# Batch 3's v as float32 from SyncE's queue, and chunk 0's output stores issued later, in a fused attention and MLP kernel

## The chip, the cores and the metric

The kernel runs on one core of a Trainium2 chip. The metric is the device time of one execution in microseconds. Three timed runs of the kernel before took 263.56, 263.73 and 264.59 us, median 263.73.

The core's engines are named as in the profile: PE (TensorE, matrix products; PEld is its weight load), DVE (VectorE), ACT (ScalarE), POOL (GpSimd) and SP (SyncE, which only issues DMAs). Each runs its own list of instructions in order and waits on semaphores of the others. POOL issues DMAs too, and only those of POOL convert float32 to bfloat16 on the way. All DMAs run on the same 16 DMA engines.

## The reference

Inputs q, k and v have the shape (8 batches, 8 heads, 576 rows, 64 columns). The attention has no product of q and k; its output is normalized and goes through an MLP with a residual:

```python
q_s = softmax(q, axis=-1)
k_s = softmax(k, axis=2)
kv = np.einsum('bhsd,bhse->bhde', k_s, v)
x = np.einsum('bhsd,bhde->bhse', q_s, kv)       # then (8, 576, 512)
xn = (x - mean(x)) / np.sqrt(var(x) + 1e-06) * g_ln
out = x + np.maximum(xn @ w_ch1, 0.0) @ w_ch2   # 512 -> 2048 -> 512
```

The output is float32.

## The kernel before

The 576 rows of a batch are split into 512 main rows (four tiles of 128) and 64 remainder rows. The work is cut into nine chunks: chunk c below 8 is the main rows of batch c, chunk 8 (`C9`) collects the remainder rows of all batches. While PE does the MLP of chunk c, the attention of batch c+1 and the loads and exponentials of batch c+2 run beside it.

**The order is written by hand.** `run` (L846) walks through the MLP steps of a chunk, `mlp_steps` (L811); each has a weight, and the running sum of weights is the position. A list of side steps, pairs of a position and a function, is merged into it: a side step is emitted when the sum reaches its position. So a position fixes where an instruction stands in its engine's list. `second_side` (L891) holds the side steps of chunk 1, `attn_fast` (L877) and `prep_fast` (L866) those of later chunks, and the loop at L1171 adds the rest. SP's DMAs, DVE's and POOL's work all follow this order.

**The MLP** of chunks from 2 on uses a scheme of seven products in place of eight (`mm1_fast`, L753, and `mm2_fast`, L684). The first layer's products are numbered; product 1 writes a PSUM bank bx, product 5 a bank bb, product 6 goes on in bx, product 2 in bc, product 7 in bx, product 3 in bb and product 4 in bx. Each is done for two groups of columns, one after the other. ACT copies bx into bc (L774) after product 1 and bb into s (L778) after product 5. DVE's L781 adds bx and s into bb after product 6; its L784 adds bx and s into hT after product 7. ACT's L792 writes the rectified results. Products 5, 6, 7 and 4 take tq as an operand: four differences of quarters of the transposed x, made two instructions each by `sum_x` (L235; L247 on POOL).

**Loads.** `load_v` (L139) loads v of a batch from POOL as bfloat16 into a tile vt of one buffer, and the remainder rows of v in two small DMAs (L149). For batch 3 it first issues a four-element copy on POOL (L143), which waits until the first pair of batch 2's x transposes has landed. `cast_v` (L131) copies half of v at a time into vm, the layout with a column of ones that the k-v product takes; DVE does it at L137, ACT at L135. `load_batch` (L1108) loads q and k on SP; for batch 3's q it waits, through a four-element conversion on POOL (L1115), until batch 2's query transposes have landed, for others through a DVE memset (L1113). q lies in the tile tag qt with two buffers in turn.

**Transposes.** `eq_T` (L259) transposes a batch's exponentiated q into eqT, and `xn_T` (L262) two of the four tiles of x at a time into xnT; both are DMA transposes on SP (L255), whose queue keeps its order.

**Stores.** `y_out` (L514) finishes a tile of chunk 0 on DVE (L518, tile ot of four buffers) and issues its store at once on POOL (L524). From chunk 1 on, `y_quarter` (L604) does the same at L609 and L615, in the same four buffers.

Of the kernel before, what the change touches and what calls it, by code (L numbers as in the profile page):

```python
# [12 lines left out]
FP32 = mybir.dt.float32  # L13
# [7 lines left out]
def kernel(  # L21
# [16 lines left out]
    nc = tc.nc  # L38
# [5 lines left out]
    T = 4  # L44
# [56 lines left out]
    def main_src(x, b, h0, hn):  # L101
        return x[b, h0 : h0 + hn, 0:SM, :].rearrange("h (p t) d -> p h (t d)", t=T)
# [28 lines left out]
    def cast_v(b, j, eng=None):  # L131
        hs = slice(4 * j, 4 * j + 4)
        dst = vm[:, b % 2, :, hs, 0:D].rearrange("p t h d -> p h t d")
        if eng is nc.scalar:
            nc.scalar.copy(dst, vts[b][:, hs])  # L135
        else:
            nc.vector.tensor_copy(out=dst, in_=vts[b][:, hs])  # L137

    def load_v(b, after=None):  # L139

        vts[b] = mlp.tile([P, H, T, D], BF16, tag="vt", name="vt", bufs=1)
        if after is not None:
            nc.gpsimd.tensor_copy(out=vts[b][0:1, 0, 0, 0:4], in_=after)  # L143
        if b == 1:
            load_krem(nc.gpsimd, b)
        nc.gpsimd.dma_start(vts[b].rearrange("p h t d -> p h (t d)"), main_src(v, b, 0, H))
        for half in range(2):
            hs = slice(4 * half, 4 * half + 4)
            nc.gpsimd.dma_start(  # L149
                vr[SR * half : SR * half + SR, b % 2, hs, 0:D],  # L150
                v[b, hs, SM:S, :].transpose([1, 0, 2]),
            )
# [340 lines left out]
    def mm1_part(c, m, t0, tn, ko):  # L493
# [13 lines left out]
        if m % 2 == 1 and at + tn == 2 and ko == KO1 - 1:  # L507
# [3 lines left out]
            else:  # L511
                nc.scalar.activation(dst, ph, AF.Relu)

    def y_out(c, t, pc, cols=slice(0, 512), eng=None):  # L514
        if cols.start == 0:
            hbox["ot"] = outp.tile([P, DM], FP32, tag="ot", name="ot")
        ot = hbox["ot"][:, cols]
        nc.vector.scalar_tensor_tensor(  # L518
            ot, in0=pc, scalar=rstds[c][:, t : t + 1], in1=xs[c][0][:, t, cols],
            op0=ALU.mult, op1=ALU.add,  # L520
        )
        eng = eng or nc.gpsimd
        if c < B:
            eng.dma_start(  # L524
                out[c, 0:SM, :].rearrange("(p t) n -> p t n", t=T)[:, t, cols], ot
            )
        else:
            for half in range(2):
                eng.dma_start(
                    out[2 * t + half, SM:S, cols], ot[64 * half : 64 * half + 64]  # L530
                )

    def mm2(c, t, ko):
        if ko == 0:
# [356 lines left out]
    def second_side():  # L891

        s = [(p, lambda i=i: quarter_w2(i, 1)) for i, p in enumerate((13, 16, 44, 46))]
        s += [(8, lambda: xn_pT(1, 2, nc.scalar)), (12, lambda: xn_pT(1, 3, nc.vector))]
        s += [(3, lambda: exp_q(2, 0, 4)), (9, lambda: exp_q(2, 2, 4)), (14, lambda: eq_T(2))]
        s += [(42, lambda: square_sum(1, 2)), (67, lambda: square_sum(1, 3)), (71, lambda: rstd_op(1))]
        s += [(14.1, lambda: load_batch(3, (2,), eqTs[2][0:1, T - 1, NP - 1, 0:4])), (31, lambda: load_batch(3, (0,)))]
        s += [(18 + 2 * j, lambda j=j: cast_v(2, j)) for j in range(2)]
        s += [(60.5, lambda: load_v(3, xnTs[2][0:1, 1, KO1 - 1, 0:4]))]
        s += [(15 + 3 * t, lambda t=t: reduce_q(2, t, 2)) for t in (0, 2)]  # L900
        s += [(36, lambda: recip_q(2))]
        s += [(18, lambda: exp_k(2, 0, 4)), (22, lambda: exp_k(2, 2, 4)), (26, lambda: prep_kvrem(2))]
        s += [(41, lambda: kv_all(2))]
        s += [(46, lambda: start_x(2))]
        for t, (p0, p1) in enumerate(((52, 54), (57, 59), (62, 65), (70, 74))):
            s += spread([lambda t=t, i=i: po_mm(2, t, i) for i in range(NP)], p0, p1)
            s += [(p1, lambda t=t: x_fast(2, t)), ((73, 82, 88, 94)[t], lambda t=t: square_sum(2, t))]
        s += [(60, lambda: xn_T(2, 0, 2)), (77, lambda: xn_T(2, 2, 2)), (100, lambda: rstd_op(2))]
        s += [(75, lambda: exp_q(3, 0, 4)), (79, lambda: exp_q(3, 2, 4)), (85, lambda: eq_T(3))]
        s += [(97, lambda: exp_k(3, 0, 4)), (108, lambda: exp_k(3, 2, 4)), (113, lambda: prep_kvrem(3))]  # L910
        s += [(p, lambda i=i: sum_w1(i, 1)) for i, p in ((2, 28), (3, 30))]
        s += spread([lambda i=i: sum_x(2, i) for i in range(4)], 95, 108)
        return s
# [207 lines left out]
    with tc.manual_schedule(  # L1121
        engines={mybir.EngineType.PE, mybir.EngineType.DVE, mybir.EngineType.Activation,
                 mybir.EngineType.SP, mybir.EngineType.Pool}
    ):
        first_batch()
        load_behind(1, (2,))
        load_w2(8, 2)
        load_behind(1, (0,))
        load_w2(10, 2)
        load_behind(1, (1,))  # L1130
        load_w2(12, 2)
        load_w2(14, 2)
        load_behind(2)

        def po_x(c, t):
            for i in range(NP):
                po_mm(c, t, i)
            x_fast(c, t)

        run(  # L1140
            mlp_steps(0),
            [
                (2, lambda: (q0_rest(2), x_fast(0, 2))),
                (2.5, lambda: (eq_pT(0, 3, nc.scalar), x_plain(0))),
                (6, lambda: (q0_rest(3), x_plain(1))),
                (7.5, lambda: (xn_pT(0, 2, nc.vector), x_fast(0, 3))),
                (16, lambda: xn_pT(0, 3, nc.vector)),
                (22, lambda: square_sum(0, 0)),
                (26, lambda: square_sum(0, 1)),
                (30, lambda: square_sum(0, 2)),  # L1150
                (34, lambda: square_sum(0, 3)),
                (38, lambda: rstd_op(0)),
            ]
            + [(70, lambda: exp_q(1, 0, 4)), (72, lambda: exp_q(1, 2, 4))]
            + [(75 + t, lambda t=t: reduce_q(1, t)) for t in range(T)]
            + [((82, 86, 94, 98)[t], lambda t=t: eq_pT(1, t, nc.scalar)) for t in range(T)]
            + [(84, lambda: nc.vector.reciprocal(eqs[1][2], eqs[1][1]))]
            + [(88, lambda: exp_k(1, 0, 4)), (92, lambda: exp_k(1, 2, 4))]
            + [(26 + 4 * i, lambda i=i: scale_w1(i % KO1, i // KO1)) for i in range(2 * KO1)]
            + [(p, lambda i=i: quarter_w2(i, 0)) for i, p in enumerate((60, 62, 64, 66))]  # L1160
            + [(p, lambda i=i: sum_w1(i, 0)) for i, p in enumerate((80, 84, 88, 92))]
            + [(p, lambda i=i: sum_w1(i, 1)) for i, p in enumerate((96, 98))]
            + [(103 + 0.4 * j, lambda j=j: cast_v(1, j)) for j in range(2)]
            + [(104.5, lambda: prep_kvrem(1))]
            + [(112, lambda: (kv_all(1), start_x(1)))]
            + [(118, lambda: (po_x(1, 0), po_x(1, 1)))]
            + [(123, lambda: xn_pT(1, 0, nc.scalar)), (125, lambda: square_sum(1, 0))]
            + [(124.1, lambda: (po_x(1, 2), po_x(1, 3)))]
            + [(126, lambda: xn_pT(1, 1, nc.scalar)), (127, lambda: square_sum(1, 1))]
        )  # L1170
        for c in range(1, B):  # L1171
            side = []
            if c == 1:
                side += second_side()
            else:
                if c + 1 < B:
                    side += attn_fast(c + 1)
                else:
                    side += attn_rest()
                    side += [(6 + i, lambda i=i: sum_x(c, i)) for i in (2, 3)]  # L1180
                if c + 2 < B:
                    side += [(1, lambda b=c + 2: load_batch(b))]
                    side += [(26, lambda b=c + 2: load_v(b))]
                    side += prep_fast(c + 2)
            if c == 2:
                side += [(19 + j, lambda j=j: cast_v(3, j)) for j in range(2)]
            if c == B - 2:
                side += [(1, load_qrem)]
                side += spread([lambda r=r: exp_qrem(r) for r in range(T)], 58, 80)
                side += [(84, lambda: eq_T(C9))]  # L1190
            sums = [(57, 0)] if c == FAST else [(p, i) for i, p in enumerate((30, 41))]
            run(mlp_steps(c), side + [(at, lambda i=i: sum_h(0, i)) for at, i in sums])
        run(mlp_steps(C9), [(33 + 3 * i, lambda i=i: sum_h(0, i)) for i in range(2)])
# [30 lines left out]
```

## Time and profile before

One execution was profiled. Its own time is 264.16 us, 0.43 above the median of the three timed runs; its span, the time that the trace covers, is 262.4 us, at a granted TensorE clock of 1.00.

| what | us |
|---|---|
| median of three timed runs | 263.73 |
| profiled execution, device time | 264.16 |
| its span | 262.4 |
| chunk 2's first product starts | 75.65 |
| batch 2's query transposes: issued, landed (8.0 later) | 51.73, 59.7 |
| batch 3's q on SP: issued, landed (5.7 later) | 60.25, 66.0 |
| batch 2's x transposes, first pair: issued, landed (7.9 later) | 63.95, 71.9 |
| chunk 0's four stores: first and last issue | 47.19, 52.38 |
| batch 3's v on POOL: issued, landed (6.4 later) | 73.28, 79.7 |

A line of a timeline gives the start in us, the time, the engine, the source line, the operation, the tiles written and read, their shapes, and how many instructions are merged. A bracket at the end gives how long the engine was idle before it, and what ended that. Rows of matmuls overlap at their ends, so how late PE is shows in the distance from start to start rather than in the busy time. For DMAs the profile has the issue, on the engine that issues (SPq, POOLq), and the time from issue to landing.

### The profile page before, as it was taken

The page shows a single profiled execution, that of the slowest core. Times are in us where ns is not written, and L with a number is a line of the kernel's source. Part 1 is how long each engine was busy: PE and PEld are TensorE (multiplying, and loading weights), DVE is VectorE, ACT ScalarE, POOL GpSimd, SP SyncE. Part 2 cuts the span into 40 slices and gives each one's busy share as a digit, 9 for nine tenths or more (in the row PEclk, how much of TensorE's full clock was granted, in tenths as well). Part 3 has the DMA queues.
Part 4 walks back from the last instruction along what each step waited for, and adds up shares of the span by engine and source line. Part 5 has one row for each costly group of instructions (what it writes and reads, how often), then busy time and mean ns, then how long its engine had stood idle before and what let it go on. Part 6 is the DMA issues. An engine that isn't in the chain of part 4 may idle for free.

```text
span 262.4 us, 6846 instructions
## 1 busy us (share of the span) xinstructions
PE 256.4 (98%) x2711; PEld 217.4 (83%) x2711; DVE 217.2 (83%) x482; ACT 180.7 (69%) x357; POOL 78.4 (30%) x130
## 2 busy tenths in 40 slices
PE   8999999999999999999999999999999999999993
PEld 5789755866888998899889988998899888888882
DVE  5676786988969997989798979997999889977873
ACT  4778670996967788678867886788678377447400
POOL 8752345200089008600860067008200300030000
PEclk9999999999999999999999999999999999999999
DMA  6999999995999964899489967997804620621014
GB/s 231 250 202 206 321 236 320 272 144 181 243 161 288 289 98 92 227 305 136 86 248 289 135 84 205 327 143 143 260 1 80 174 74 5 77 104 58 0 42 120
DMA packets 69895, 45.00 MB, mean 172 GB/s; under 512 B 41508, under 2 KB 66088, under 8 KB 69864
## 3 DMA queue, kind: packets, MB, share of 16 engines
q0 software_dynamic: 20368, 22.29, 38.8%
q1 hardware_dynamic: 48896, 21.76, 38.7%
q10 hardware_dynamic: 600, 0.53, 0.6%
q8 instruction: 21, 0.34, 0.5%
q14 instruction: 10, 0.08, 0.1%
HBM read 36.70 MB, written 9.44 MB: 176 GB/s over the span
## 4 chain that ended last, share of the span: by engine, by line
PE 92%; DMA 3%; POOL 1%; DVE 1%; issue 1%; ACT 0%; POOLq 0%; DVEq 0%
PE ba L598 19%; PE bx L750 18%; PE bb L750 9%; PE ph L501 8%; PE pc L547 5%; PE bc L750 5%; PE bc L598 5%; PE be L598 5%; PE bb L598 5%; DMA xnT<-xn 3%; PE ph L486 3%; PE warm L864 3%; PE po L417 2%; PE pkv L381 2%; PE ptr L933 1%
## 5 line engine op out<-in xcount | busy, mean ns | idle before, releaser
L598 PEld LDWEIGHTS <-hs 128*128 128x128 bf16 x512 | 49.6, 98 | 5.7
L750 PEld LDWEIGHTS <-w_q 128*128 128x128 bf16 x448 | 43.1, 98 | 5.6 <-issue 0.7
L598 PEld LDWEIGHTS <-hT 128*128 128x128 bf16 x392 | 37.3, 98 | 4.4
L750 PEld LDWEIGHTS <-w1g 128*128 128x128 bf16 x336 | 32.3, 98 | 4.0
L247 POOL TENSOR_TENSOR tq<-xnT 128x256 bf16<-128x256 bf16 x20 | 13.0, 666 | 64.4 <-DMA xnT<-xn 48.9
L598 PE MATMUL ba<-w_q,hs 128*128 128x256 bf16 x256 | 31.7, 273 | 0.0
L750 PE MATMUL bx<-tq,w_q 128*128 128x256 bf16 x224 | 29.0, 273 | 0.2 <-ACT s L778 0.2
L615 POOL DMA_DIRECT2D out_dram<-ot x28 | 15.3, 555 | 45.9 <-DVE ot L609 45.9
L431 ACT ACTIVATE scrap<-x,mv 128x512 bf16<-128x512 bf16 x36 | 26.0, 721 | 1.8 <-DVE x L447 1.4
L447 DVE SCALAR_TENSOR_TENSOR x<-po,rq 128x512 bf16<-128x512 f32 x34 | 23.3, 684 | 1.3 <-PE po L417 1.2
L774 ACT COPY bc<-bx 128x512 f32<-128x512 f32 x28 | 15.2, 595 | 13.0 <-PE bx L750 13.0
L781 DVE TENSOR_TENSOR bb<-bx,s 128x512 f32<-128x512 f32 x28 | 18.2, 694 | 6.8 <-ACT s L778 6.7
L792 ACT ACTIVATE hT<-bc 128x512 bf16<-128x512 f32 x28 | 15.3, 595 | 12.0 <-PE bc L750 12.0
L209 DVE TENSOR_REDUCE zq<-eq 128x16 f32<-128x1024 bf16 (+1 forms) x20 | 20.8, 1051 | 1.3 <-ACT eq L192 1.2
L578 DVE TENSOR_TENSOR hs<-hT 128x1024 bf16<-128x1024 bf16 x32 | 20.9, 674 | 0.9 <-ACT hT L792 0.5
L792 ACT ACTIVATE hT<-bb 128x512 bf16<-128x512 f32 x28 | 15.2, 595 | 8.4 <-PE bb L750 8.4
L784 DVE TENSOR_TENSOR hT<-bx,s 128x512 bf16<-128x512 f32 x28 | 18.1, 684 | 2.9 <-PE bx L750 2.9
L417 PE MATMUL po<-kv_sb,eqT 128*128 128x128 bf16 x120 | 20.2, 219 | 0.0
L623 ACT COPY s<-ba 128x512 f32<-128x512 f32 x15 | 8.7, 579 | 11.9 <-PE ba L598 7.3
L598 PE MATMUL ba<-w_sb,hT 128*128 128x256 bf16 x128 | 16.7, 273 | 0.0
L598 PE MATMUL bb<-w_q,hs 128*128 128x256 bf16 x128 | 16.5, 273 | 0.0
L778 ACT COPY s<-bb 128x512 f32<-128x512 f32 x28 | 15.6, 622 | 0.6 <-PE bb L750 0.5
(150 smaller groups left out, 543.8 us busy)
## 6 DMA issues: line engine op xcount, KB each, us to landing
out_dram<-ot POOLq DMA_DIRECT2D x32, 256.0 KB, 6.0
qt<-in_q_dram SPq DMA_DIRECT2D x5, 1024.0 KB, 6.9
kt<-in_k_dram SPq DMA_DIRECT2D x5, 1024.0 KB, 13.5
vt<-in_v_dram POOLq DMA_DIRECT2D x7, 512.0 KB, 13.4
qt<-in_q_dram POOLq DMA_DIRECT2D x2, 1024.0 KB, 12.6
kt<-in_k_dram POOLq DMA_DIRECT2D x2, 1024.0 KB, 14.7
kt<-in_k_dram SPq DMA_DIRECT2D x4, 288.0 KB, 4.6
w_raw<-in_moe_w_ch_dram POOLq DMA_DIRECT2D x4, 256.0 KB, 9.2
```

The lines of the kernel that those rows point to most:

```text
L209: nc.vector.reduce_sum(eqs[c][1][:, ts], eqs[c][0][:, ts], axis=AX.X)
L417: nc.tensor.matmul(pobox["p"][:, i * P : i * P + P], eqTs[c][:, t, i, :], kv_sb[:, c, i, :], start=True, stop=True,)
L431: nc.scalar.activation(scrap, x[:, t], AF.Square, bias=mv[:, t, 0:1], scale=-float(DM), accum_out=mv[:, t, 1:2],)
L447: nc.vector.scalar_tensor_tensor(x[:, t].rearrange("p (h d) -> p h d", h=H), in0=pobox[c, t].rearrange("p (h d) -> p h d", h=H), scalar=1. ...
L501: nc.tensor.matmul(ph[:, m % 2, at : at + tn], (w1g if c else w1_sb)[:, ko, m * P : (m + 1) * P], xnTs[c][:, t0 : t0 + tn, ko, :], start=( ...
L578: nc.vector.tensor_tensor(out=dst, in0=x, in1=y, op=op)
L598: nc.tensor.matmul(dst, lhsT, rhs, start=first and (own or t == 0) and k == 0, stop=k == KH - 1, skip_group_check=True)
L750: nc.tensor.matmul(dst[:, q], lhsT, rhs, start=first and q == 0 and ko == 0, stop=ko == 1, skip_group_check=True)
L778: nc.scalar.copy(at[g, "s"], at[g, "b"])
L781: nc.vector.tensor_tensor(out=at[g, "b"], in0=at[g, "x"], in1=at[g, "s"], op=ALU.add)
L784: nc.vector.tensor_tensor(out=h_out(g, 1, 1), in0=at[g, "x"], in1=at[g, "s"], op=ALU.add)
L792: nc.scalar.activation(h_out(g, odd, half), at[g, name], AF.Relu)
```

## The change

It has four parts.

- Batch 3's v is no longer loaded by `load_v` on POOL. `load_v32` loads it as float32 on SP, at position 78 of chunk 1, behind the second pair of x's transposes (position 77), into a tile of the tag qt. That tag's two buffers go round one place further for the later batches. The four-element copy on POOL goes.
- The two remainder loads of batch 3's v stay on POOL, in a function of their own, and are issued at position 14.3 of chunk 1 in place of 60.5.
- The casts of batch 3's v, both on DVE at positions 19 and 20 of chunk 2, come at position 4 on DVE and 10 on ACT, from float32.
- Chunk 0's four stores are held back in a list and issued on POOL at position 14.2 of chunk 1, right behind the conversion (14.1) that waits for batch 2's query transposes.

```diff
-    def load_v(b, after=None):
+    def load_v(b):
         vts[b] = mlp.tile([P, H, T, D], BF16, tag="vt", name="vt", bufs=1)
-        if after is not None:
-            nc.gpsimd.tensor_copy(out=vts[b][0:1, 0, 0, 0:4], in_=after)
         if b == 1:
             load_krem(nc.gpsimd, b)
         nc.gpsimd.dma_start(vts[b].rearrange("p h t d -> p h (t d)"), main_src(v, b, 0, H))
+        load_vrem(b)
+
+    def load_v32(b):
+        vts[b] = raw.tile([P, H, T, D], FP32, tag="qt", name="vt32")
+        nc.sync.dma_start(vts[b].rearrange("p h t d -> p h (t d)"), main_src(v, b, 0, H))
+
+    def load_vrem(b):
         for half in range(2):
...
+    late = []
+
     def y_out(c, t, pc, cols=slice(0, 512), eng=None):
...
-        if c < B:
+        if c == 0:
+            late.append((t, ot))
+        elif c < B:
...
+    def store_late():
+        for t, ot in late:
+            nc.gpsimd.dma_start(
+                out[0, 0:SM, :].rearrange("(p t) n -> p t n", t=T)[:, t, :], ot
+            )
...
-        s += [(60.5, lambda: load_v(3, xnTs[2][0:1, 1, KO1 - 1, 0:4]))]
+        s += [(14.2, store_late), (14.3, lambda: load_vrem(3)), (78, lambda: load_v32(3))]
...
-                side += [(19 + j, lambda j=j: cast_v(3, j)) for j in range(2)]
+                side += [(4, lambda: cast_v(3, 0)), (10, lambda: cast_v(3, 1, nc.scalar))]
```

## The prediction

> **What bounds the kernel now.** I read the page's busy times first, then the chain that ended last, and then the timelines of each engine around the one place where TensorE (PE) is late.
>
> ```profile
> span 262.4 us, 6846 instructions
> PE 256.4 (98%) x2711; PEld 217.4 (83%) x2711; DVE 217.2 (83%) x482; ACT 180.7 (69%) x357; POOL 78.4 (30%) x130
> PE 92%; DMA 3%; POOL 1%; DVE 1%; issue 1%; ACT 0%; POOLq 0%; DVEq 0%
> ```
>
> PE is busy 98% of the span at full granted clock, and 92% of the chain is PE. So a change to loads and stores can gain only where PE is late, and it loses wherever it makes PE late anew. The timeline of PE shows the late place, at the start of chunk 2:
>
> ```profile
> 75.65 1.04 PE L750 MATMUL bx<-xnT,w1g 128*128 128x256 bf16 x8
> 76.83 1.03 PE L750 MATMUL bb<-tq,w_q 128*128 128x256 bf16 x8
> 78.07 1.03 PE L750 MATMUL bx<-tq,w_q 128*128 128x256 bf16 x8 [0.21 <-ACT s L778]
> 78.94 1.04 PE L750 MATMUL bc<-xnT,w1g 128*128 128x256 bf16 x8
> ...
> 81.56 1.16 PE L750 MATMUL bx<-tq,w1g 128*128 128x256 bf16 x8
> 82.56 0.27 PE L750 MATMUL bx<-xnT,w1g 128*128 128x256 bf16 x1
> ```
>
> The first column is the start. Undisturbed, a row of eight follows the last after 0.87 us (78.07 to 78.94; in chunk 3, 102.66 to 103.53). Here the steps are 1.18, 1.24 and 1.00 us: PE loses 0.31, 0.37 and 0.13, together **0.81 us**. Elsewhere after 60 us PE's rows join, but for about 0.2 us around each batch's small attention matmuls, which stays. POOL's timeline names the cause of the first two:
>
> ```profile
> 71.98 0.18 POOL L143 COPY vt<-xnT 1x4 bf16<-1x4 bf16 x1 [11.76 <-DMA xnT<-xn]
> 73.28 0.91 POOL L146 DMA_DIRECT2D vt<-in_v_dram  x1 [1.12 <-issue]
> 74.18 1.28 POOL L149 DMA_DIRECT2D vr<-in_v_dram  x2
> 75.44 1.34 POOL L247 TENSOR_TENSOR tq<-xnT 128x256 bf16<-128x256 bf16 x2
> 76.71 1.31 POOL L247 TENSOR_TENSOR tq<-xnT,tq 128x256 bf16<-128x256 bf16 x2
> ```
>
> Product 5 multiplies by tq's first difference, ready at 76.78, and starts at 76.83; product 6 by the second, ready at 78.02, and starts at 78.07. PE's bracket names ACT's L778, but product 6 does not write the bank that L778 copies; the dates fit POOL. POOL was late because, from the landing of x's first transposes (72.0), it issued batch 3's v for 3.4 us before the differences. The third loss, 0.13, is VectorE's (DVE's): its cast of v (81.06, 0.42 us) stands ahead of the second L784, which ends at 82.07; product 4 of group 1 restarts at 82.13.
>
> **The change, part by part.**
>
> *v's load leaves POOL.* Gone ahead of the differences are the copy and its gap (1.30 us from 71.98 to 73.28), the load's issue (0.91) and two remainder issues (1.28). What is late next is the second pair of x's transposes: issued when the first issue ends at 68.9 and landing 3.7 us later (DMA issues by window), 72.7. From there, at 1.27 us a difference, the four are ready at 73.9, 75.2, 76.5 and 77.8. PE wants them at 76.5, 77.4, 79.15 and 80.9 (75.65 plus 1, 2, 4 and 6 rows of 0.875). Slack is 2 us or more even if the transposes land no earlier. Gain 0.68 us.
>
> *Chunk 0's four stores move.* Their issues (0.54 to 0.57 us each, 2.2 us) go from 47.2–52.9 to behind POOL's cast that waits for batch 2's query transposes (59.75), with v's remainder issues (1.28) behind them; POOL then has nothing until 72. Those transposes now land 8.0 us after issue beside the stores; the next two sets of that size take 4.3 each. So I expect them at about 56.0 in place of 59.7, and batch 3's q, k and the stores all to start some 3.7 us earlier. The stores put 1 MB beside q's and k's 2 MB: at some 330 GB/s (the DMA view from 62 us on) that is 3 us more, so the queue ahead of x's transposes empties about when it does now, or 1 us sooner. q is read by ACT at 66.45 and lands at 66.0; started 3.7 us earlier with at most 3 us of store traffic in the way, it is in time. The store tiles are written again by L609 at 70.73; issued at 56.5 to 58.7 and landing 6.0 to 8 us later, they are free. Cost zero; without that cover see rival C.
>
> *v in float32 on SP's queue.* One issue (0.4 us) behind the second pair of x's transposes, whose issue ends at 70.6 or sooner. Behind it on SP stand batch 3's query transposes (70.71 now, first read by PE at 87.8), then q, k and k's remainder of batch 4, which wait for DVE until 77.8 anyway; 1 MB more (3 us) is covered by over 9 us. Landing: q's 1 MB loads took 5.7 us (issued 60.25) and 6.9 (issued 77.9), so v is there by 76.3 to 77.5. The buffer taken is q's of batch 2, read out by ACT at 51.7; batch 4's q goes to the other, which batch 3's q leaves at 68.4. The cast now asks for v at 77.86.
>
> *The casts.* DVE's two (0.42 and 0.47, at 81.06 and 82.45) go: that returns 0.13. One comes at position 4, behind the memsets, into this hole:
>
> ```profile
> 76.64 1.21 DVE L209 TENSOR_REDUCE zq<-eq 128x16 f32<-128x1024 bf16 x1
> 77.79 0.06 DVE L1113 MEMSET qt<- 1x1 f32 x1
> 77.79 0.06 DVE L1113 MEMSET kt<- 1x1 f32 x1
> 78.76 1.30 DVE L781 TENSOR_TENSOR bb<-bx,s 128x512 f32<-128x512 f32 x2 [0.91 <-ACT s L778]
> ```
>
> No row has DVE copy float32 to bf16 from SBUF. The bounds are 0.42 (the bf16 copy of 1024) and 1.20 (the reduction of 1024). I take 0.68, the 1024-element bf16 TENSOR_TENSOR of L561, because it reads as many bytes per element. Queued behind it are L781's two adds, and product 7 of each group writes the bank that they read. With POOL on time they would be ready at 78.09 (chunk 3: 105.10 less 102.66, plus 75.65). The cast holds them to 78.5; they end at 79.2 and 79.8; product 7 wants its banks at 79.15 and 79.59, and restart takes 0.06 (82.07 to 82.13). That is 0.11 plus 0.16, **0.27 us lost**. At 0.42 it is 0.02; at 1.20 it is 0.80.
>
> *ACT's cast* is 1.06 us (ACT's 1024-element float32 exponential). It falls after its L778 pair, ending in chunk 3 2.69 us after the first product: 78.3 to 79.4. ACT's next work, L792, starts at 79.64 today, so the wait for PE there covers it; uncovered it would cost up to 1.06 us.
>
> **Sum:** 0.68 + 0.13 − 0.27 = 0.54 us less. PE's instructions stand in the same order in both kernels, so nothing else moves, and every later stage is PE-bound and slides forward. The profiled execution took 264.16 us (span 262.4 and 1.8 around it): 263.6. The median of the three timed runs is 263.73, 0.43 below the profiled one, so I predict 263.2. With the ends for the cast the gain is 0.79 or 0.01: 262.9 to 263.7.
>
> **A lock between POOL and DVE.** POOL's conversion at 59.75 took 0.47 us for four elements, where its copy of four at 71.98 took 0.18; it ran beside DVE's two-input L561 and ended within 0.05 us of it. The Trainium skill, SBUF — State Buffer, section "SBUF: two separate sides", says that a Vector operation in a two-port mode, which a float32 copy in SBUF is said to trigger, and a GpSimd operation exclude each other for the whole instruction, the later one waiting. That single row agrees with the rule for a two-input operation; DVE's bf16 copy at 82.45 took only 0.04 longer beside a POOL issue. By the rows alone: if the last difference still runs at 77.86 and the cast waits it out, up to 0.66 us (one L247) is added; this is part of rival A.
>
> **Rivals.**
>
> A. *The late engine becomes DVE.* The cast takes 1.20, or it waits for POOL, so L781 is as late as POOL was. For: the hole is 0.91 us and shrinks when POOL is on time. Against: POOL should be done by 77.8. Results: 263.7 for 1.20; 0.68 plus 0.66 costs 0.27 + 0.66 = 0.93 against the 0.81 gained, 263.9.
>
> B. *v lands late, slower.* DVE's cast stands still on the DMA and everything behind it on DVE, then PE, waits one for one. It decides from a landing at 78.4 (the gain is gone) and passes 0.5% at 79.7. For: k's 1 MB issued at 78.4 took 13.1 us, behind q and beside stores; from 70.6 that is 83.7, 5.8 us late: 269. Against: nothing as large is in front of v, only the transposes. A middle case, landing at 80, is 265.3.
>
> C. *It doesn't do what it says.* If the query transposes stay at 59.7, the stores (60.2 to 62.4) stand among q and k, q lands up to 3 us later, and ACT stalls at 66.45 by about 2.5; its copies of PE's banks (69.05) run late by as much, some 1.3 us of which reaches PE. The transposes land after 75.2, and the differences are late again: 264 to 265.1.
>
> **Chances.** Forecast 0.60; A 0.20 (0.10 for a cast of 1.20, 0.10 for the wait on POOL); B 0.10, of which 0.08 is past the bound; C 0.07, of which 0.03; other gains 0.03, for which I see no room, since only 0.81 us is there. The bound is 0.5% (1.3 us), about what a measurement of this kernel can tell from no change: faster 0.03, same 0.86, slower 0.11. The range reaches from the full 0.81 and some spread (the timed runs span 1.0 us) to A and the milder part of C: 262.6 to 264.5.
>
> **What would show it.** Right: L247 starts at 71 to 73 with no DMA issue in front; PE's rows of 75 to 83 us follow at 0.87 with at most 0.3 us lost before product 7; batch 2's query transposes land 4 to 5 us after issue. Wrong: DVE idle before its cast with v's DMA as releaser (B); a cast over 0.9 us (A); ACT idle before L192 on q's DMA (C).

## The result and the profile after

The changed kernel takes **264.69 us** (median of 17 runs, 264.18 to 266.03), the kernel before 263.99 (17 runs, 263.56 to 264.60). The ratio is 1.0029, 95% interval 1.0017 to 1.0041: slower by 0.70 us, where 0.54 us faster was forecast. That is inside the 0.5% that the prediction calls no change, but outside its range (262.6 to 264.5).

The profiled execution took 266.03 us, the slowest of the 17, with a span of 263.6. So its own numbers are read as one sample, and medians are compared for the total. The page of the changed kernel:

```profile
span 263.6 us, 6840 instructions
PE 256.1 (97%) x2708; PEld 217.3 (82%) x2711; DVE 217.6 (83%) x481; ACT 181.6 (69%) x358; POOL 77.0 (29%) x128
PE 86%; DMA 6%; DVE 3%; POOL 1%; issue 1%; ACT 0%; SPq 0%; POOLq 0%; DVEq 0%
```

PE's share of the chain fell from 92% to 86%, DVE's rose from 1% to 3%. PE's timeline at the start of chunk 2 says where:

```profile
76.54 1.04 PE L766 MATMUL bx<-xnT,w1g 128*128 128x256 bf16 x8
77.42 1.05 PE L766 MATMUL bb<-tq,w_q 128*128 128x256 bf16 x8
78.31 1.04 PE L766 MATMUL bx<-tq,w_q 128*128 128x256 bf16 x8
79.18 1.04 PE L766 MATMUL bc<-xnT,w1g 128*128 128x256 bf16 x8
81.12 1.19 PE L766 MATMUL bx<-tq,w_q 128*128 128x256 bf16 x8 [0.90 <-DVE bb L797]
82.15 1.04 PE L766 MATMUL bb<-xnT,w_q 128*128 128x256 bf16 x8
```

(L766 and L797 are L750 and L781 of the kernel before.) The waits before products 5 and 6 are gone: the steps are 0.88, 0.89, 0.87. In their place stands a step of 1.94 us, 1.07 lost before product 7, plus 0.15 within it; 0.16 more is lost at 74.80. DVE's timeline names the new wait:

```profile
78.89 0.06 DVE L1129 MEMSET kt<- 1x1 f32 x1
79.32 1.14 DVE L137 CAST vm<-vt 128x1024 bf16<-128x1024 f32 x1 [0.37 <-DMA vt<-in_v_dram]
80.37 1.28 DVE L797 TENSOR_TENSOR bb<-bx,s 128x512 f32<-128x512 f32 x2
```

The cast waits 0.37 us for v and takes 1.14 instead of the 0.68 assumed. POOL's and SP's timelines give the dates (the SP rows: issue, time to the end of the issue):

```profile
57.66 0.18 POOL L1131 CAST qt<-eqT 1x4 f32<-1x4 bf16 x1 [12.36 <-DMA eqT<-eq]
58.21 2.18 POOL L545 DMA_DIRECT2D out_dram<-ot  x4 [0.37 <-issue]
60.38 1.29 POOL L155 DMA_DIRECT2D vr<-in_v_dram  x2
74.84 1.30 POOL L253 TENSOR_TENSOR tq<-xnT 128x256 bf16<-128x256 bf16 x2 [13.17 <-DMA xnT<-xn]
...
78.61 1.29 POOL L253 TENSOR_TENSOR tq<-xnT,tq 128x256 bf16<-128x256 bf16 x2
79.85 2.35 POOL L631 DMA_DIRECT2D out_dram<-ot  x4
```

```profile
52.47 3.25 SPq L261 DMA_TRANSPOSE eqT<-eq  x1
57.86 0.40 SPq L117 DMA_DIRECT2D qt<-in_q_dram  x1
...
64.51 8.20 SPq L261 DMA_TRANSPOSE xnT<-xn  x2
72.81 0.53 SPq L150 DMA_DIRECT2D vt<-in_v_dram  x1
```

Batch 2's query transposes land 5.1 us after issue (8.0 before), as forecast. But x's transposes are issued no earlier (64.51) and take 8.2 us to issue (6.7 before), so the differences run from 74.84 to 79.9 (forecast: ready by 77.8) and v is issued at 72.81 (forecast: 70.6 at the latest), landing at 79.3.

**And 0.6 us lie outside the span.** The device time less the span is 1.80 us on average in the runs of the kernel before (1.74 to 1.86) and 2.41 in those of the changed kernel (2.37 to 2.47). The median spans, 261.95 to 262.2 in the groups of runs before and 262.3 after, differ by only 0.1 to 0.35.

### The profile page after: what moved, and what is told of

It reads as the page before. It is cut to its first block, busy times and chain, and to the rows that moved or that the text cites. A ratio compares the mean times of both kernels' runs of the same rounds, so it can differ in the third digit from the quotient of the medians.

```text
span 263.6 us, 6840 instructions
## 1 busy us (share of the span) xinstructions
PE 256.1 (97%) x2708; PEld 217.3 (82%) x2711; DVE 217.6 (83%) x481; ACT 181.6 (69%) x358; POOL 77.0 (29%) x128
## 4 chain that ended last, share of the span: by engine, by line
PE 86%; DMA 6%; DVE 3%; POOL 1%; issue 1%; ACT 0%; SPq 0%; POOLq 0%; DVEq 0%
PE ba L614 18%; PE bx L766 18%; PE bb L766 9%; PE ph L507 8%; PE pc L563 5%; PE be L614 5%; PE bc L614 5%; PE bb L614 5%; PE bc L766 5%; DMA qt<-in_q_dram 4%; PE ph L492 3%; DMA vt<-in_v_dram 2%; PE po L423 2%; PE pkv L387 2%; DVE hs L594 1%; PE ptr L949 1%
## 5 line engine op out<-in xcount | busy, mean ns | idle before, releaser
L766 PEld LDWEIGHTS <-w_q 128*128 128x128 bf16 x448 | 43.0, 98 | 6.2 <-DVE bb L797 1.2
L766 PEld LDWEIGHTS <-w1g 128*128 128x128 bf16 x336 | 32.2, 98 | 3.9
L766 PE MATMUL bx<-tq,w_q 128*128 128x256 bf16 x224 | 29.2, 273 | 0.9 <-DVE bb L797 0.9
L797 DVE TENSOR_TENSOR bb<-bx,s 128x512 f32<-128x512 f32 x28 | 18.2, 694 | 6.0 <-ACT s L794 5.8
L808 ACT ACTIVATE hT<-bc 128x512 bf16<-128x512 f32 x28 | 15.3, 594 | 10.8 <-PE bc L766 10.8
L808 ACT ACTIVATE hT<-bb 128x512 bf16<-128x512 f32 x28 | 15.2, 595 | 9.3 <-PE bb L766 9.3
## 6 DMA issues: line engine op xcount, KB each, us to landing
kt<-in_k_dram SPq DMA_DIRECT2D x5, 1024.0 KB, 14.3
kt<-in_k_dram POOLq DMA_DIRECT2D x2, 1024.0 KB, 14.4
```

The source lines that it names most:

```text
L766: nc.tensor.matmul(dst[:, q], lhsT, rhs, start=first and q == 0 and ko == 0, stop=ko == 1, skip_group_check=True)
L797: nc.vector.tensor_tensor(out=at[g, "b"], in0=at[g, "x"], in1=at[g, "s"], op=ALU.add)
L808: nc.scalar.activation(h_out(g, odd, half), at[g, name], AF.Relu)
```

## The experiments

Two questions: what of the 0.70 us is chunk 2's (stores, cast), and what is the program's end. The theory after the result was that the late stores and the cast's wait take back the gain, and that the time outside the span is a cost of its own. The rival was that the late cast explains all of it. Times are medians, and ratios are to the kernel before on the same chip; a kernel is called by the first part of its name (e1, p2); "loses" is PE's distance from start to start beyond a step's normal one, in the profiled execution.

**Chunk 2: stores and cast.** Each is one edit; the second is to the kernel before, the others to the changed one.

```diff
# e1_stores_at_once
-        if c == 0:
-            late.append((t, ot))
-        elif c < B:
+        if c < B:
...
-        s += [(14.2, store_late), (14.3, lambda: load_vrem(3)), (78, lambda: load_v32(3))]
+        s += [(14.3, lambda: load_vrem(3)), (78, lambda: load_v32(3))]
# e2_stores_only (kernel before, with late.append and store_late added)
+        s += [(14.2, store_late)]
# e3_cast_at_19
-                side += [(4, lambda: cast_v(3, 0)), (10, lambda: cast_v(3, 1, nc.scalar))]
+                side += [(19, lambda: cast_v(3, 0)), (10, lambda: cast_v(3, 1, nc.scalar))]
# e6_both_on_ACT
-                side += [(4, lambda: cast_v(3, 0)), (10, lambda: cast_v(3, 1, nc.scalar))]
+                side += [(24, lambda: cast_v(3, 0, nc.scalar)), (10, lambda: cast_v(3, 1, nc.scalar))]
```

> The changed kernel with one part undone: chunk 0's stores are issued at once, as before the change; v on SP in float32 and the two early casts stay. Theory 1 (the stores, moved among batch 3's q and k, hold up SP's queue: x's second transposes landed at 74.8 in place of 72.7 us and v at 79.3): v is issued by 71 us and lands at 76 to 77.5, DVE's cast does not wait for it, ACT does not wait for k, and PE loses only what the cast costs, 0.3 to 0.8 us at product 7; ratio to before 0.998 to 1.000. Theory 2 (the place and length of the cast alone, 1.14 us in a hole of 0.9): product 7 waits as long as in the changed kernel but for the 0.37 us of DMA wait, 0.8 us, ratio 1.000 to 1.002. Side question, the cast's 1.14 us: if a POOL difference that overlapped it held it up, it is about 0.7 here, since POOL is done by 77.8; if float32 is read one element a cycle, it stays 1.1.

Measured: 264.93 against 263.77, ratio 1.0036 (1.0022 to 1.0050), outside the span 2.44. In its profile the differences come at 72.97, the cast takes 0.70 and PE loses 0.15 in chunk 2:

```profile
76.74 1.29 POOL L253 TENSOR_TENSOR tq<-xnT,tq 128x256 bf16<-128x256 bf16 x2
77.98 2.28 POOL L629 DMA_DIRECT2D out_dram<-ot  x4
```

```profile
78.37 0.70 DVE L137 CAST vm<-vt 128x1024 bf16<-128x1024 f32 x1
```

The differences are over at 78.0, ahead of the cast: chunk 2 behaves as forecast, and yet the total is not better. The time is outside the range of both theories. So the late stores aren't the whole loss.

> The kernel before with one part of the change alone: chunk 0's stores held back until batch 2's query transposes have landed; v stays on POOL in bfloat16 with its casts at 19 and 20. Theory 1: x's transposes land about 2 us later than in the kernel before, so POOL's four-element copy, v's issue and the differences start 2 us later, and PE loses about 2 us more at products 5 and 6: ratio 1.006 to 1.009, slower than the changed kernel. Theory 2: stores matter little, ratio 0.999 to 1.002.

Measured: 264.45, ratio 1.0024 (1.0005 to 1.0043), outside 1.81. The time lies between the two theories' ranges: with v still on POOL, the late stores alone are slower. In the one profile POOL's copy behind x's first transposes starts at 72.47 (71.98 before) and the differences at 75.92 (75.44 before); PE loses 1.08 and 0.37 at products 5 and 6:

```profile
75.37 1.04 PE L760 MATMUL bx<-xnT,w1g 128*128 128x256 bf16 x8
77.31 1.03 PE L760 MATMUL bb<-tq,w_q 128*128 128x256 bf16 x8 [0.91 <-POOL tq L247]
78.56 1.03 PE L760 MATMUL bx<-tq,w_q 128*128 128x256 bf16 x8 [0.21 <-ACT s L788]
```

But the differences start anywhere from 73.25 to 76.41 in the five profiles with v on POOL and early stores (the kernel before, e4, p2, p3, p4; the last four are introduced below). So this profile doesn't show that the stores made them late.

> The changed kernel with DVE's cast of batch 3's v moved back from position 4 to position 19 (the other half stays on ACT at 10, the stores stay late). Theory 1: the wait of 1.07 us before product 7 goes, because DVE's adds no longer stand behind v's landing; DVE's cast comes behind the first L800 and costs product 4 of group 1 0.4 us if it takes 0.7, 0.8 us if it takes 1.1; the wait of ACT for k (0.86 us) and PE's 0.16 us at 74.8 stay. Ratio to before 0.998 to 1.001. Theory 2: the same but with no trace of k's lateness, ratio 0.997. The cast's length: 0.7 if POOL's differences were what held it, 1.1 if not.

Measured: 264.71, ratio 1.0036 (1.0024 to 1.0048). The cast takes 0.69 at 80.80, where POOL only issues DMAs; PE loses 0.40 at the second group's product 4 and nothing before it in chunk 2. The stage is as theory 1 has it, the time is not (1.001 at most).

> The changed kernel with both casts of batch 3's v on ACT, at positions 10 and 24 (stores stay late). Both theories: DVE is free of casts, so product 7 waits only if ACT is late; ACT's first cast is ready after its L794 pair, about 79.3, and holds the rectified copies of bc to 80.4, which nothing waits for at once. Theory 1: v's lateness (79.3) costs nothing, PE's loss of chunk 2 falls from 1.2 us to 0.2 us or less, and the ratio to before is 0.997 to 0.999. A loss of more than 0.5 us would show that ACT's queue is as tight as DVE's there.

Measured: 264.38, ratio 1.0025 (1.0016 to 1.0034). ACT's casts take 1.10 and 1.06; PE loses 0.59 at 83.07, waiting for ACT's L808: more than the 0.5 that was to show ACT's queue to be as tight as DVE's. None of the four cures the kernel; all three with v on SP have 2.3 to 2.4 us outside the span.

**The lock on the cast.** Probe copies in the kernel before, in chunk 4:

```diff
+        def probe():
+            dst = mlp.tile([P, 2, T, D], BF16, tag="probe", name="probe", bufs=1)
+            nc.vector.tensor_copy(out=dst, in_=raws[6][2][:, 0:2])
...
+            if c == 4:
+                side += [(p, probe) for p in (45, 62, 101, 102, 103)]
```

> The kernel before with five probe copies on DVE in chunk 4, each of 512 elements from float32 to bfloat16 (half the size of the cast in question; they write a tile that nothing reads). Two stand where POOL computes nothing, three where POOL's differences L247 run. Theory: DVE's copy from float32 takes 0.70 us for 1024 elements and is held up by a POOL computation that runs at the same time, which made 1.14 us of it. Then the two free probes take about 0.35 us, and those that meet an L247 take longer, up to 0.66 more, and end with it. Rival: the 1.14 us had nothing to do with POOL (DMA writes into the same tile, say); then all five take the same time. The device time is not asked for.

Measured: 0.42 us each, but for the one that met L247 (two of the three meant to meet it came before it). DVE's and POOL's rows:

```profile
139.63 0.42 DVE L1137 CAST probe<-qt 128x512 bf16<-128x512 f32 x1
...
144.94 0.42 DVE L1137 CAST probe<-qt 128x512 bf16<-128x512 f32 x1
...
151.40 0.88 DVE L1137 CAST probe<-qt 128x512 bf16<-128x512 f32 x2
...
152.79 0.63 DVE L1137 CAST probe<-qt 128x512 bf16<-128x512 f32 x1
153.34 0.86 DVE L609 SCALAR_TENSOR_TENSOR ot<-be,rstd,x 128x256 f32<-128x256 f32 x2
```

```profile
152.47 1.48 POOL L247 TENSOR_TENSOR tq<-xnT 128x256 bf16<-128x256 bf16 x2 [17.84 <-DMA xnT<-xn]
153.91 1.29 POOL L247 TENSOR_TENSOR tq<-xnT,tq 128x256 bf16<-128x256 bf16 x2
```

The probe that started at 152.79 took 0.21 longer, and the pair of L247 beside it 0.19 longer than the next pair: each waited for the other. L609, which reads PSUM, ran beside the next L247 at no cost to it (1.29).

**The end of the program.** In the trace's own records SP waits at the end for every semaphore of the DMAs in a fixed order, about 0.062 us a step (start, duration, what is waited for). The kernel before:

```
 260.734  0.028 Sync  EVENT_SEMAPHORE  $S[101]>= $S[114]>=
 260.796  0.028 Sync  EVENT_SEMAPHORE  $S[103]>= $S[113]>=
 ...
 261.164  0.028 Sync  EVENT_SEMAPHORE  $S[118]>= $S[106]>=
```

The changed kernel:

```
 262.298  0.028 Sync  EVENT_SEMAPHORE  $S[101]>= $S[114]>=
 ...
 262.727  0.028 Sync  EVENT_SEMAPHORE  $S[118]>= $S[106]>=
```

PE's last matmul starts at 257.715 in the first and at 259.076 in the second, so the first wait of the row is over 3.02 us after it in the one and 3.22 in the other.

SP's and ACT's DMAs take eight semaphores in turn (101, 103, 104, 105, 107, 108, 117, 118). The last two stores use 118 (ACT) and 101 (SP) in the kernel before, 101 (ACT) and 103 (SP) in the changed one, which has one SP DMA more. The first wait of the row, for 101, is then for ACT's store, which is issued later than SP's, and all the other waits come behind it: SP's waits are over 3.51 us after PE's last matmul in the kernel before and 3.72 in the changed one. Kernels with idle instructions added or one load moved:

```diff
# p2_sp_pad: kernel before, in chunk 4 (p3_sp_pad_x3: three, p4_sp_pad_x8: eight)
+        nc.sync.dma_start(pad[0:1, 0:4], q[0, 0, 0:1, 0:4])
# p1_pool_pads: e1_stores_at_once, in chunk 4
+        for i in range(3):
+            nc.gpsimd.memset(pad[0:1, 4 * i : 4 * i + 4], 0.0)
# p5_one_load_to_POOL: e1_stores_at_once; b0_changed_end_mended: the changed kernel
-            load_krem(nc.sync, b)
+            load_krem(nc.sync, b, (0, 1) if b < B - 1 else (0,))
...
+        if b == B - 1:
+            load_krem(nc.gpsimd, b, (1,))
# b1_end_mended_cast_19: p5 with the cast of e3; b2_late_stores_cast_19: b0 with it
# b3_turn_one_less: b1, with both halves of batch 7's load_krem on POOL
# c1_end_mended_pool_pad: b0, c2_late_cast_19_pool_pad: b2, each with one memset on POOL
+        nc.gpsimd.memset(pad[0:1, 0:4], 0.0)
```

> The changed kernel with chunk 0's stores issued at once, and three memsets of four elements added on POOL in chunk 4 where it is idle, so that POOL has as many instructions as in the kernel before. Asked is the device time outside the profile's span, which was 1.81 us in the kernel before and 2.45 us in this kernel without the three. Theory that POOL's shorter program brings the extra time: it goes back to about 1.8 us, and the median to 0.6 us below e1_stores_at_once, 264.3 us or less. Rival, that SP's additional DMA brings it: it stays at 2.45 us.

> The kernel before with one more DMA on SP, of 16 bytes, in chunk 4. Theory that SP's additional DMA brings the extra time outside the span: it goes from 1.81 to about 2.4 us, and the median is 0.6 us above the kernel before. Rival, that POOL's shorter program (the copy and one DMA issue fewer) brings it: it stays at 1.81 us, and the median within 0.2 us of the kernel before.

> The kernel before with three more DMAs of 16 bytes on SP in chunk 4 (p2_sp_pad had one). Theory: one more SP DMA shifts by one place which of the eight semaphores the last output stores signal; at the end SP waits for the semaphores in a fixed order, 0.062 us each, so that its chain from TensorE's last instruction to the end of the span goes from 4.65 to 4.86 us with one; with three it is about 4.7 to 4.75. And the time outside the span, 2.16 us with one, stays near 2.16 if it is a step that SP's longer program passes once. Rival: the cost is by the DMA; then the time outside is 2.8 us or more.

> The kernel before with eight more DMAs of 16 bytes on SP in chunk 4: a full turn of the eight semaphores, so the last stores signal the same ones as in the kernel before. Theory of the turn: from TensorE's last instruction to the end of the span 4.65 us again. For the time outside the span: 2.16 us if it is a step that SP's longer program passes, 1.81 if it too goes by the turn of the semaphores, 4.6 if it is by the DMA.

> The changed kernel with chunk 0's stores issued at once (e1_stores_at_once), and one of SP's two loads of the last rows of batch 7's k (64 KB) issued on POOL instead, so that SP has as many DMAs as in the kernel before. Theory that SP's additional DMA takes back what the stage gains: the stage keeps its 0.64 us, the chain from TensorE's last instruction to the span's end and the time outside it lose 0.5 to 0.6 us together against e1_stores_at_once, and the median comes 0.3 to 0.6 us below the kernel before. Rival, that v's 1 MB on SP's queue itself brings the time at the end: it stays at that of e1_stores_at_once, 0.5 us or more above the kernel before.

Measured. The columns: DMAs on SP and ACT, and instructions on POOL, against the kernel before (POOL's by the trace's records); from the start of PE's last matmul to the end of the span, in the profiled execution; outside the span, mean of the runs; their sum; median and ratio to the kernel before beside it.

| kernel | SP, ACT | POOL | in span | outside | sum | median us | ratio (95%) |
|---|---|---|---|---|---|---|---|
| before | 0 | 0 | 4.65 | 1.80 | 6.45 | 263.99 | |
| after | +1 | −3 | 4.55 | 2.41 | 6.96 | 264.69 | 1.0029 (1.0017–1.0041) |
| e1 | +1 | −3 | 4.55 | 2.44 | 6.99 | 264.93 | 1.0036 (1.0022–1.0050) |
| e2 | 0 | 0 | 4.75 | 1.81 | 6.56 | 264.45 | 1.0024 (1.0005–1.0043) |
| p1 | +1 | 0 | 4.97 | 2.10 | 7.07 | 264.66 | 1.0022 (1.0004–1.0040) |
| p2 | +1 | 0 | 4.85 | 2.16 | 7.01 | 264.39 | 1.0020 (1.0003–1.0036) |
| p3 | +3 | 0 | 4.79 | 2.18 | 6.97 | 264.88 | 1.0042 (1.0026–1.0059) |
| p4 | +8 | 0 | 4.70 | 1.81 | 6.51 | 263.77 | 1.0006 (0.9991–1.0022) |
| p5 | 0 | −1 | 4.71 | 2.09 | 6.80 | 264.17 | 1.0002 (0.9989–1.0015) |
| b0 | 0 | −1 | 4.70 | 2.07 | 6.77 | 264.38 | 1.0022 (1.0011–1.0033) |
| b1 | 0 | −1 | 4.70 | 2.08 | 6.78 | 265.07 | 1.0041 (1.0025–1.0056) |
| b2 | 0 | −1 | 4.69 | 2.08 | 6.77 | 264.31 | 1.0017 (1.0003–1.0031) |
| b3 | −1 | 0 | 4.49 | 2.01 | 6.50 | 264.21 | 1.0010 (0.9997–1.0023) |
| c1 | 0 | 0 | 4.72 | 1.99 | 6.71 | 264.52 | 1.0030 (1.0016–1.0044) |
| c2 | 0 | 0 | 4.71 | 1.99 | 6.70 | 264.19 | 1.0005 (0.9994–1.0015) |

One 16-byte DMA on SP lengthens the end of the kernel before by 0.56 us (p2), three by 0.52 (p3); eight, a full turn, by 0.06 (p4). The part in the span is from one profile each; with the semaphores of the kernel before and v on POOL it reads 4.65 to 4.75 (before, e2, e4, p4), so differences under 0.1 say nothing. That shows the place in the turn, not the number of DMAs, as a cause. 0.20 of the 0.56 is SP's row of waits (over 3.71 after the last matmul, 3.35 in b3), and 0.35 lies outside the span, where the trace has no instructions: which engine is late there isn't shown. p1's and p2's theories each explained half of what they were to explain (2.10 for 1.8, 2.16 for 2.4); p3 and p4 fit the turn. p5 was a miss: its end is 0.19 shorter than e1's, not 0.5 to 0.6, and it comes out level with the kernel before, not below. POOL's three missing instructions bring nothing: p1, which restores them, has 0.34 less outside and 0.42 more inside the span than e1, and its median, 264.66, is not the 264.3 or less of its theory.

> The changed kernel whole, stores late and all, with one of SP's two loads of the last rows of batch 7's k issued on POOL, so that the count of DMAs on SP and with it the semaphores of the last stores are those of the kernel before. Theory that the shifted semaphores are the larger part of the loss: 0.5 to 0.75 us come off, to 264.0 to 264.2 us, level with the kernel before; outside the span 2.1 us, of which 0.3 has only moved out of it. Rival, that the loss is in chunk 2 and by the late stores: not more than 0.35 comes off, 264.35 or more.

> p5_one_load_to_POOL with DVE's cast of v at position 19 in place of 4, behind L784, where POOL computes nothing. Theory of the lock: DVE's cast takes 0.70 us in place of 1.14, the second and third L781 are not late, and TensorE loses up to 0.4 us at the second group's product 4 in place of 0.6 at product 7: 0.2 to 0.3 us less than p5_one_load_to_POOL, and 0.1 to 0.3 below the kernel before. Rival: DVE has no slack at 19 either, and the time stays at that of p5_one_load_to_POOL.

> b0_changed_end_mended with DVE's cast at position 19. Against b1_end_mended_cast_19 it differs only in the late stores. Theory that the late stores cost by delaying x's transposes, q and k, and win by making batch 2's query transposes early, for which TensorE waited 0.82 and 1.28 us at 61 us in two of the profiles of kernels with early stores: then query transposes land by 58 and that wait is gone, while x's transposes come 2 us later; net between 0.3 us less and 0.3 us more than b1_end_mended_cast_19.

> b1_end_mended_cast_19 with both of the loads of the last rows of batch 7's k on POOL, so that SP has one DMA less than the kernel before and the last stores signal the semaphores one place earlier in the turn (ACT's last on the seventh in place of the eighth, SP's last on the eighth in place of the first). Theory of SP's chain of waits: 0.18 us less to the end of the span. For the time outside the span: it stays at 2.1 if only a store at the turn's begin is dear, and rises by 0.35 if any place but that of the kernel before is.

Measured: 264.38, 265.07, 264.31 and 264.21. b0's profile has chunk 2 as forecast (DVE's cast 0.71 at 78.03, PE losing 0.15), and its end is 0.19 shorter than the changed kernel's. But of the 0.5 to 0.75 only 0.31 came off, which is on the rival's side of the line, by 0.03 us. b1 was a miss: the cast took 0.69 and PE lost 0.40, as expected, yet it is 0.9 us slower than p5. Its profile has PE waiting at 61 us for batch 2's query transposes, beside which the early stores run:

```profile
61.53 0.23 PE L425 MATMUL po<-kv_sb,eqT 128*128 128x128 bf16 x1 [1.30 <-DMA eqT<-eq]
```

This wait stands in 3 of the 10 profiles with early stores (p2 0.82, p5 1.28, b1 1.47 us lost; the transposes land at 60.77 to 61.49) and in none of the 8 with late ones (landing at 56.13 to 57.60). Why b1 as a whole is slower than p5 isn't settled by one profile of each. b2 was a miss too: it is 0.76 below b1, where 0.3 either way was expected; its cast took 0.87 and PE lost 0.57 in chunk 2. b3's span is 0.2 shorter at the end, as expected, and outside it 2.01, between the two expectations.

> b0_changed_end_mended with one memset of four elements on POOL in chunk 4, so that POOL too has as many instructions as in the kernel before. From the end of SP's waits to the end of the execution the kernel before and two others with its counts take 2.95 us, all kernels with other counts 3.15 to 3.3, b0 (POOL one short) 3.24. Theory that it goes by the counts on POOL and SP together: 2.95 again, 1.8 outside the span, and the median 0.3 us below b0_changed_end_mended's 264.38, 264.1 or less. Rival, that something else of the changed program sets it: the time stays at 264.4.

> b2_late_stores_cast_19 with the same memset on POOL: the changed kernel with the end of the program as before, and DVE's cast behind L784. Theory of the counts: 0.3 us below b2_late_stores_cast_19's 264.31, about 264.0, level with the kernel before; rival: it stays at 264.3.

Measured: 264.52, a miss, and 264.19. Outside the span it is 1.99, not 1.81: the pad gave back 0.08, and about 0.2 of the changed program's end stays unexplained. One rival was not run: every kernel with v on SP also has at least one cast less on DVE and one more on ACT. In e6, with both casts on ACT, 2.31 lies outside the span where e3 has 2.42, and 4.55 inside in both. So the counts on SP and POOL aren't all that sets it, but that doesn't show where the 0.2 comes from. c1's profile has the cast beside POOL again (1.23 us), and PE loses 0.91 in chunk 2. c2 is level with the kernel before (ratio 1.0005), as p5 is (1.0002), and 0.5 us better than the changed kernel; no version beat the kernel before.

## Why the prediction was wrong

**The failed step is "nothing else moves", with the "1.8 around it" that was carried over unchanged.** SP's additional DMA was priced at its issue and its bytes, not at which semaphore the last stores signal. The end of the execution grew from 6.45 to 6.96 us, 0.51 of the 0.70 us. p2, p3 and p4 show that the turn alone can cost that much in the kernel before. In the changed program, b0, with the turn restored, takes 0.19 off, and 0.3 stays that c1 only reduced by 0.06; between p1 and c1, which both have POOL's count of the kernel before, it is 0.36. So for the changed program itself the turn is shown for part, and the rest is open. The time came out 1.24 us from the forecast (0.70 slower in place of 0.54 faster): 0.51 of that is the end, about 0.4 the gain that chunk 2 didn't bring (below), and 0.3 is open.

**"Gain 0.68": right in mechanism.** With no DMA issue in front of the differences, the first products 5 and 6 waited in none of the 12 profiles with v on SP; in the six with v on POOL they lost 0 to 1.45 us (0.68 in the one that the forecast used). But that 0.68 was one sample: the five profiles of the kernel before and its padded copies lost 0.25 to 1.71 us between 57 and 84 us, mean 0.90 (0.82, 1.71, 1.15, 0.25, 0.58).

**"Cost zero" for the stores: not settled.** The query transposes did land early: 4.6 to 5.1 us after issue in all eight profiles with late stores, 6.5 to 9.6 in nine with early ones (the tenth has no landing), and the wait at 61 us, which the profile of before did not show, is in none of the eight. What follows is not clearly later for it. With v on SP the first difference starts at 72.53 to 74.84 us in the seven profiles with late stores (74.84 in the changed kernel, 73.11 and 74.42 in b0 and c1, whose stage is the same) and at 72.97 to 75.28 in the five with early ones. Four pairs differ in the stores alone. By the ratios in the table, late stores are slower by 0.0024 (e2 against the kernel before) and 0.0020 (b0 against p5), and faster by 0.0007 (the changed kernel against e1) and 0.0024 (b2 against b1). So with v on SP no cost of the stores is shown.

**"I take 0.68" for the cast: the size is right, its neighbour wrong.** Free of POOL's computation it takes 0.69 or 0.70 (e1, e3, b1, b3, c2; 0.87 in b2, unexplained). Beside a whole difference it takes 1.12 to 1.23 (after, p1, p5, c1) and ends 0.55 to 0.57 us after that does; in b0 it meets only the last 0.16 us of one and takes 0.71. This is the wait that rival A held at 0.10, and with it v's landing (79.3 where 76.3 to 77.5 was forecast) as a small part of B. The step under it is "POOL should be done by 77.8": that date came from one profile's landing of x's second transposes, 72.7. In the 12 profiles with v on SP they land at 72.39 to 75.14, and the last difference ends at 77.59 to 80.35. The Trainium skill, SBUF — State Buffer, section "SBUF: two separate sides", says that a Vector operation in a two-port mode and a GpSimd operation exclude each other for the whole instruction; the probe's 0.63 against 0.42, with L247 held up in its turn, agrees with it.

**"0.27 us lost" at product 7** was 1.22 in the changed kernel's profile (1.07 and 0.15), 0.91 in c1 and 0.15 in b0. With the 0.16 at 74.80 the three lose 1.38, 0.91 and 0.15, mean 0.81, against 0.90 with v on POOL. So chunk 2 gained about 0.1 on average where 0.54 was forecast; with three and five profiles that spread over more than a microsecond, this is an estimate. ACT's cast (1.06 to 1.10) was covered, as forecast.

**What stays open:** 0.51 from the end less 0.1 from chunk 2 is 0.4 of 0.70. In the six profiles with v on POOL chunk 1's k–v products start at 56.51 to 56.86 us (mean 56.7), in the 12 with v on SP at 56.65 to 57.59 (mean 57.1), although no instruction of the change stands before 47 us. Ten of the 12 are later than the latest of the six. In four of the five latest (c1, after, b3, e3) ACT waits 1.29 to 1.60 us for the second half of batch 0's q, which lands at 13.9 to 14.4 us there and at 12.4 to 13.1 in the others. That would be the missing 0.3 to 0.4, but no run was made for it, and whether the change brings it or chance between executions is open.

## What to carry to other kernels

Price a change of a fraction of a percent against the end of the program too: look at which semaphores the last stores signal, at SP's row of waits, and at the device time less the span, since one more DMA on SP moved them by 0.56 us here. Before a single profile's stall is booked as gain, ask how much it varies: here the same stall was 0 to 0.97 us in the five profiles of the kernel before and its padded copies. And place a DVE copy from float32 in SBUF where POOL doesn't compute: beside a difference it took 1.12 to 1.23 us here, and 0.69 or 0.70 free of one (once 0.87).

## What was not expected of the hardware

- One DMA of 16 bytes on SP, over 120 us before the end, cost 0.56 us at the end (p2), eight cost 0.06 (p4).
- POOL's DMA issues did not hold up DVE's float32 copy (0.69 to 0.71 beside them in e1, e3, b0, b1, b3 and c2), but for 0.87 in b2; POOL's computation did (1.12 to 1.23). The other way round the copy held up issues: the first of chunk 1's four store issues took 0.73 beside it (after, p1, p5, b0, c1) and 0.60 free of it, the last 0.83 to 0.95 (b1, b3, c2) in place of 0.54 or 0.55; in e1 and e3 hardly.
- Batch 2's query transposes took 8.0 us from issue to landing beside the stores in the kernel before and 5.1 with the stores behind them in the changed one.
